# Retention and two MLPs on one core: the constants' load moves from SyncE's queue to ScalarE's

## The chip, the cores and the metric

The kernel runs on one core of one Trainium2 chip. The metric is the device time of one execution, in microseconds (us). Three runs of the kernel before took 550.88, 551.44 and 550.36 us; the median is 550.88 us. A further execution was profiled, and all rows below come from that one.

## The reference, cut to what matters

A decaying linear attention ("retention") runs over 2 batches, 8 heads, 768 steps of width 64. Its output, reshaped to 1536 tokens by 512, goes through two MLPs of width 2048.

```python
gamma = 1.0 - 2.0 ** (-5.0 - np.arange(H))           # one decay per head
for t in range(S):
    state = gamma * state + einsum('bhd,bhe->bhde', k[:, :, t], v[:, :, t])
    y[:, :, t] = scale * einsum('bhd,bhde->bhe', q[:, :, t], state)
x = y.transpose(0, 2, 1, 3).reshape(B * S, H * D)
h = x @ w_in                                          # first MLP
x = (h * tanh(softplus(h))) @ w_out
h = x @ w_in2                                         # second MLP
out = (h * cos(h)) @ w_out2
```

## The kernel before, in words

The retention is cut into 6 chunks of 128 steps, each for both batches. For a chunk TensorE (PE) forms the scores of queries against keys (`att_scores`, L465), VectorE (DVE) multiplies them by a decay mask (`att_mask`, L469, tile `p`), and PE multiplies the result by the values (`att_out`, L506). A running state joins the chunks (`att_update` L479, `att_state` L490, `att_inter` L516); its values come scaled from ScalarE (ACT) and GpSimd (POOL) (`att_vd`, L447 and L444, tile `vd`). ACT then writes the high part of the chunk's output (L526) and a copy of it (L535), and DVE the low part (L538). Everything after that, from 44 us of the trace on, is the matmuls of the two MLPs, each done in three products of high and low parts (L621, L579, L649).

The masks are not loaded. A small tensor of 184 numbers a partition, `consts`, is loaded into the tile `few` (L1040), and the tables of powers grow from it by doublings: DVE makes the mask of 128 x 1024 (`att_mask_grow`, L1051 and L1054, then `att_mask_upper`, L1064), POOL copies the decays that `vd` needs (`att_dec`, L1067) and grows the table for the queries (`att_decq_grow`). All of that waits for the landing of `few`. Beside it, from 1.06 us on, PE runs 24 matmuls on zeros (`start_up`, `zeros`, L1075) ahead of the first scores.

All transfers were issued on SyncE's queue (SP), in a fixed order: `few` first, then queries and keys of chunk 0 (one transfer for each batch, 512 KB), its values (256 KB for each batch), queries and keys of chunk 1, and so on (`chunk_loads`, L419). A transfer waits, on SP, for the landing of the one eight places ahead of it. ACT's first instruction is a table load that the first activation (L1082) brings with it.

The order of the rest is worked out when the program is built: `Plan` holds each operation with a cost and what it needs, goes through them from the end and from the start, and emits the instructions of each engine in the order of the best of 12 rounds. Operations with the engine `None` take no time in it; in the rounds, SP's first operation begins at 2.6, and another engine may use a transfer 2.2 after its operation's end. So the cost and the place that `load_consts` is given there decide when the plan believes the mask and the loads to be there.

Of the kernel before, what the change touches and what calls it, by code (L numbers as in the profile page):

```python
# [88 lines left out]
class Plan:  # L89
# [24 lines left out]
    def op(self, engine, cost, fn, *args, needs=(), uses=(), new=None):  # L114
        n = len(self.ops)
        uses = list(uses)
        before = set(needs)
        reuse = []
        for key, bufs, *tag in [] if new is None else new if isinstance(new, list) else [new]:
            line = self.lines.setdefault(tag[0] if tag else key[0], [])  # L120
            if line:
                before.add(self.owner[line[-1]])
            if len(line) >= bufs:
                reuse.append(line[-bufs])
            line.append(key)
            self.owner[key] = n
            uses.append(key)
        for key in uses:
            if self.owner.get(key, n) != n:
                before.add(self.owner[key])  # L130
            self.users.setdefault(key, set()).add(n)
        if engine in self.given:
            before |= {self.last[engine]} if engine in self.last else set()
            self.last[engine] = n
        att = fn.__name__.startswith("att") or fn.__name__ in ("start_up", "zeros", "load_consts")
        self.ops.append(dict(engine=engine, cost=cost, fn=fn, args=args, before=before, reuse=reuse, att=att, due=(fn.__name__, *args[:1]) in self.DUE or (fn.__name__,) in self.DUE))
        return n
# [125 lines left out]
def retention_two_mlps(ctx: ExitStack, tc: tile.TileContext, qkv, w1i, w1o, w2i, w2o, consts, out):  # L263
    nc = tc.nc
# [476 lines left out]
    op = plan.op  # L741
# [295 lines left out]
    def load_consts():  # L1037
        t = g_p.tile([128, 2, 2, BLK], F32R, tag="g2", name="few").rearrange("p a b c -> p (a b c)").bitcast(F32)
        few_t.append(t)
        nc.sync.dma_start(out=t[:, 0:184], in_=consts[:, 0:184])  # L1040
        upper = t[:, 512 : 512 + C]
        nc.gpsimd.memset(upper, 1.0)
        nc.gpsimd.affine_select(
            out=upper, in_=upper, pattern=[[1, C]], compare_op=ALU.is_ge, fill=0.0, base=0, channel_multiplier=-1
        )
# [38 lines left out]

    at["close"] = op(None, 0.0, nothing)
    at["ret"] = op(None, 0.0, nothing)
    op("PE", 5.5, start_up)
    load = op("SP", 0.4, load_consts, new=("few", 1, "g2"))
    qk, v, k = (0, 1024), (1024, 1536), (1536, 2048)
    for c, cuts in (  # L1090
        (0, qk), (0, v), (1, qk), (0, k), (1, v), (2, qk), (1, k), (3, qk), (2, v), (2, k), (4, qk), (3, v), (3, k),
# [209 lines left out]
```

## Time and profile before

| | |
|---|---|
| median of three runs | 550.88 us (550.36 to 551.44) |
| the profiled execution's own time | 551.34 us |
| its span, first to last instruction | 549.6 us |
| PE busy | 543.3 us (99%) |
| DVE, ACT, POOL busy | 395.3, 315.7, 195.7 us |
| granted TensorE clock | 0.999 of full speed |
| bytes moved | 49.33 MB, mean 90 GB/s |

The profiled execution is 1.74 us longer than its span; that is what lies around the first and last instruction. All three engines beside PE have idle time, PE has 6.3 us of it. The rows further down show where in the span that idle time lies, and what the transfers do at the start. A row's time is counted from the span's start.

### The profile page before, as it was taken

The page shows a single profiled execution, that of the slowest core. Times are in us where ns is not written, and L with a number is a line of the kernel's source. Part 1 is how long each engine was busy: PE and PEld are TensorE (multiplying, and loading weights), DVE is VectorE, ACT ScalarE, POOL GpSimd, SP SyncE. Part 2 cuts the span into 40 slices and gives each one's busy share as a digit, 9 for nine tenths or more (in the row PEclk, how much of TensorE's full clock was granted, in tenths as well). Part 3 has the DMA queues.
Part 4 walks back from the last instruction along what each step waited for, and adds up shares of the span by engine and source line. Part 5 has one row for each costly group of instructions (what it writes and reads, how often), then busy time and mean ns, then how long its engine had stood idle before and what let it go on. Part 6 is the DMA issues. An engine that isn't in the chain of part 4 may idle for free.

```text
span 549.6 us, 7462 instructions
## 1 busy us (share of the span) xinstructions
PE 543.3 (99%) x2962; PEld 451.8 (82%) x2962; DVE 395.3 (72%) x450; ACT 315.7 (57%) x423; POOL 195.7 (36%) x171
## 2 busy tenths in 40 slices
PE   9989999999999999999999999999999999999997
PEld 7888888888888888888888888888888888888886
DVE  5789997776676756385798893978487884978452
ACT  4475646264323404334188978899577867686460
POOL 6772205536341316143223324441514333422000
PEclk9999999999999999999999999999999999999999
DMA  8982420242222220241001312042202301020103
GB/s 287 410 347 78 154 76 1 76 153 78 76 78 76 78 76 2 76 154 40 38 0 43 130 58 76 1 153 78 77 1 78 134 20 76 1 77 1 76 35 118
DMA packets 16162, 49.33 MB, mean 90 GB/s; under 512 B 1792, under 2 KB 2176, under 8 KB 16128
## 3 DMA queue, kind: packets, MB, share of 16 engines
q1 hardware_dynamic: 16128, 48.86, 23.7%
q8 instruction: 23, 0.38, 0.3%
q14 instruction: 11, 0.09, 0.0%
HBM read 45.71 MB, written 3.15 MB: 89 GB/s over the span
## 4 chain that ended last, share of the span: by engine, by line
PE 95%; DVE 1%; DMA 1%; ACT 1%; issue 0%; SPq 0%; DVEq 0%; ACTq 0%
PE bank L649 48%; PE bank L579 26%; PE bank L621 18%; PE bank L506 2%; DMA qkv<-qkv_dram 1%; PE bank L465 1%; PE bank L516 1%; PE bank L479 1%; DVE p L469 0%; ACT vd L447 0%; DVE x L538 0%; DVE mag L334 0%; ACT y L535 0%; ACT x L526 0%; SPq L419 0%
## 5 line engine op out<-in xcount | busy, mean ns | idle before, releaser
L649 PE MATMUL bank<-g,wo 128*128 128x512 f32 x576 | 134.0, 389 | 0.0
L649 PE MATMUL bank<-wo,g 128*128 128x512 f32 (+1 forms) x588 | 133.5, 385 | 0.0
L649 PEld LDWEIGHTS bank<-wo,g 128*128 128x128 f32 x588 | 108.9, 188 | 22.0
L649 PEld LDWEIGHTS bank<-g,wo 128*128 128x128 f32 x576 | 108.1, 188 | 22.4
L621 PE MATMUL bank<-x,wi 128*128 128x512 f32 x432 | 99.4, 389 | 0.0
L621 PEld LDWEIGHTS bank<-x,wi 128*128 128x128 f32 x432 | 81.0, 188 | 16.9 <-issue 0.2
L579 PE MATMUL bank<-x,wi 128*128 128x512 f32 x270 | 66.1, 389 | 0.0
L579 PE MATMUL bank<-S,T 128*128 128x512 f32 x270 | 66.1, 389 | 0.0
L374 POOL TENSOR_TENSOR raw<-mag 128x512 f32<-128x512 f32 x14 | 19.4, 1385 | 127.2 <-DVE mag L355 53.5
L719 DVE TENSOR_TENSOR acc<-bank,acc 128x1024 f32<-128x1024 f32 x35 | 42.7, 1221 | 28.9 <-PE bank L649 28.9
L363 POOL TENSOR_TENSOR wo<-mag,wo 128x512 fp32r<-128x512 f32 x28 | 37.7, 1368 | 71.8 <-ACT wo L349 71.8
L703 DVE TENSOR_TENSOR g<-bank,g 128x1024 fp32r<-128x1024 f32 x40 | 48.9, 1222 | 18.0 <-ACT g L699 17.8
L579 PEld LDWEIGHTS bank<-x,wi 128*128 128x128 f32 x270 | 50.6, 188 | 10.6
L579 PEld LDWEIGHTS bank<-S,T 128*128 128x128 f32 x270 | 50.7, 188 | 10.5
L587 ACT COPY U<-bank 128x512 f32<-128x512 f32 x45 | 26.5, 589 | 54.9 <-PE bank L579 54.7
L392 POOL TENSOR_TENSOR T<-raw,T 128x512 fp32r<-128x512 f32 x28 | 36.5, 1327 | 51.8 <-ACT T L388 51.8
L363 POOL TENSOR_TENSOR wi<-mag,wi 128x512 fp32r<-128x512 f32 x28 | 42.6, 1535 | 32.6 <-ACT wi L349 27.0
L656 ACT ACTIVATE bank<-bank 128x1024 f32<-128x1024 f32 x24 | 24.2, 1009 | 47.5 <-PE bank L621 32.1
L692 DVE TENSOR_TENSOR bank<-angle,bank 128x512 f32<-128x512 f32 (+1 forms) x32 | 30.7, 959 | 28.4 <-ACT angle L688 28.2
L590 DVE TENSOR_TENSOR bank<-bank,U 128x512 f32<-128x512 f32 x45 | 31.3, 697 | 26.3 <-PE bank L579 26.1
L699 ACT CAST g<-bank 128x1024 fp32r<-128x1024 f32 x40 | 40.7, 1016 | 9.3 <-DVE bank L692 8.7
L674 DVE SCALAR_TENSOR_TENSOR angle<-bank,angle 128x512 f32<-128x512 f32 (+1 forms) x32 | 30.5, 953 | 19.9 <-ACT angle L670 19.4
(90 smaller groups left out, 651.9 us busy)
## 6 DMA issues: line engine op xcount, KB each, us to landing
raw<-w1i_dram SPq DMA_DIRECT2D x16, 512.0 KB, 4.1
raw<-w1o_dram SPq DMA_DIRECT2D x16, 512.0 KB, 3.6
raw<-w2i_dram SPq DMA_DIRECT2D x16, 512.0 KB, 3.7
raw<-w2o_dram SPq DMA_DIRECT2D x16, 512.0 KB, 3.7
qkv<-qkv_dram SPq DMA_DIRECT2D x12, 512.0 KB, 7.4
qkv<-qkv_dram SPq DMA_DIRECT2D x22, 256.0 KB, 7.0
out_dram<-acc SPq DMA_DIRECT2D x11, 256.0 KB, 2.0
out_dram<-acc SPq DMA_DIRECT2D x2, 128.0 KB, 1.7
```

The source lines that it names most:

```text
L363: eng.tensor_sub(out=w[:, :, 1], in0=w_all_of(it, single)[:, ns].bitcast(F32), in1=w[:, :, 0].bitcast(F32))
L392: nc.gpsimd.tensor_sub(out=t[:, :, 1], in0=t_of(it)[:, part], in1=t[:, :, 0].bitcast(F32))
L579: nc.tensor.matmul(ps, lhs, rhs, start=(not more and kk + i == 0), stop=(kk == 1 and i == last), skip_group_check=True)
L587: nc.scalar.copy(out=copies[0][:, n], in_=bank[:, WINO_BANK["d"], :])
L590: nc.vector.tensor_add(out=bank[:, WINO_BANK[to], :], in0=bank[:, WINO_BANK[of], :], in1=copies[0][:, n])
L621: nc.tensor.matmul(h, w[:, f % 2, a, kk * 128 : (kk + 1) * 128], x[:, b, kk, :], start=(a + b + kk == 0), stop=(a == 1 and kk == KD - 1),)
L649: nc.tensor.matmul(ps, lhs, rhs, start=(n == 0), stop=(n == 3 * GF - 1))
L674: nc.vector.scalar_tensor_tensor(out=a, in0=h, scalar=INV_2PI, in1=a.bitcast(I32), op0=ALU.mult, op1=ALU.subtract)
L692: nc.vector.tensor_mul(out=h, in0=a, in1=h)
L699: nc.scalar.copy(out=g_t[k][:, :, 0, :], in_=h_of(k))
L703: nc.vector.tensor_sub(out=g[:, :, 1, :], in0=h_of(k), in1=g[:, :, 0, :].bitcast(F32))
L719: nc.vector.tensor_add(out=acc, in0=o_of((m * NG + G, j, p)), in1=acc)
```

## The change

`load_consts` issues the load of `few` on ACT's queue instead of SP's. In the plan it becomes an operation without an engine and without a cost, ahead of `start_up`, which is made to need it; ACT issues the transfer ahead of its first activation. The operation on SP that the consumers of `few` wait for stays in the plan as an empty one of cost 0.0.

```diff
     def load_consts():
...
-        nc.sync.dma_start(out=t[:, 0:184], in_=consts[:, 0:184])
+        nc.scalar.dma_start(out=t[:, 0:184], in_=consts[:, 0:184])
         upper = t[:, 512 : 512 + C]
...
-    op("PE", 5.5, start_up)
-    load = op("SP", 0.4, load_consts, new=("few", 1, "g2"))
+    first = op(None, 0.0, load_consts, new=("few", 1, "g2"))
+    op("PE", 5.5, start_up, needs=[first])
+    load = op("SP", 0.0, nothing, uses=["few"])
```

On ACT, at the start of the program (`few` is the tile of the constants, `spare` and `quarter` are single columns that only serve to bring the table):

```order
-L1296 UNCONDITIONAL_BRANCH [waits barrier_Pool_Activation_PE_DVE_SP_release]
+L1297 UNCONDITIONAL_BRANCH [waits barrier_Pool_Activation_PE_DVE_SP_release]
+L1040 DMA few<-consts_dram 128x184
 L1082 ACT_TABLE_LOAD
 L1082 ACTIVATE spare<-quarter 128x1 [waits DVE_49]
```

ACT now issues the transfer before its table load, and waits for nothing but the barrier at the program's start.

On SP, at the start of the program (`qkv` of 128x1024 is queries and keys of chunk 0 for one batch, of 128x512 its values):

```order
-L1296 UNCONDITIONAL_BRANCH [waits barrier_Pool_Activation_PE_DVE_SP_release]
-L1040 DMA few<-consts_dram 128x184
+L1297 UNCONDITIONAL_BRANCH [waits barrier_Pool_Activation_PE_DVE_SP_release]
 L419 DMA qkv<-qkv_dram 128x1024 x2
 L419 DMA qkv<-qkv_dram 128x512 x2
```

Every load of `qkv` moves up by one place; the order among them is the same.

On DVE, in the stretch in which the first MLP begins (`mag` and `raw` are steps in splitting a weight, `x` is the low part of an output of the last chunks):

```order
 L355 SCALAR_TENSOR_TENSOR raw<-raw,mag 128x512 [waits DVE_49]
 L318 TENSOR_SCALAR mag<-raw 128x512 [waits DMAHW5_49]
+L324 TENSOR_SCALAR mag<-mag 128x512 [waits DVE_49]
 L538 TENSOR_TENSOR x<-bank,x 128x4x128 [waits DMAHW3_49,DMAHW1_49,DMAHW7_49,DMAHW0_49,Activation_49]
-L324 TENSOR_SCALAR mag<-mag 128x512 [waits DVE_49]
 L328 TENSOR_SCALAR mag<-mag 128x512 [waits DVE_49]
 L363 TENSOR_TENSOR wi<-raw,wi 128x512 [waits Activation_49]
```

One clamp of a weight (L324) now stands ahead of one low part of `x` (L538). PE's and POOL's orders are the same as before.

## Rows read from the trace of the kernel before

**Rows 1.** The page's head, and its chain that ended last, by engine.

```profile
span 549.6 us, 7462 instructions
PE 95%; DVE 1%; DMA 1%; ACT 1%; issue 0%; SPq 0%; DVEq 0%; ACTq 0%
```

**Rows 2.** Stretches: start:end, length, busy us by engine, clock, DMA share, GB/s.

```profile
0.00:15.00 15.00, 13.78 (x170) 11.22 (x172) 9.30 (x22) 6.67 (x19) 9.79 (x21) 1.00 0.86 297
15.00:44.00 29.00, 27.23 (x573) 24.30 (x567) 23.35 (x38) 15.67 (x45) 20.65 (x20) 1.00 0.87 342
44.00:100.00 56.00, 56.00 (x251) 46.40 (x248) 51.37 (x67) 32.12 (x39) 15.59 (x12) 1.00 0.23 84
100.00:300.00 200.00, 200.00 (x884) 165.62 (x883) 137.09 (x135) 82.94 (x97) 75.07 (x59) 1.00 0.18 67
300.00:500.00 200.00, 200.00 (x883) 165.53 (x882) 151.31 (x167) 157.26 (x204) 72.02 (x58) 1.00 0.19 69
```

**Rows 3.** The chain that ended last, its beginning: start us, us, what.

```profile
0.81 0.37 SPq L1040
...
1.24 0.41 SPq L419
...
2.17 6.41 DMA qkv<-qkv_dram
...
8.66 2.02 ACT vd L447 x8
...
12.11 0.49 ACT y L535
...
14.43 1.29 DVE p L469 x2
...
15.77 1.09 PE bank L506 x14
```

**Rows 4.** Timeline of the first 17 us, all engines: start us, us, instruction, [idle before].

```profile
0.80 1.28 ACT L1082 ACT_TABLE_LOAD   x1 [0.80 <-PEq L1290]
...
2.10 0.30 ACT L1082 ACTIVATE spare<-quarter 128x1 f32<-128x1 f32 x1
2.75 0.17 DVE L1051 COPY cst<-few 128x8 f32<-128x8 f32 x1 [1.73 <-DMA few<-consts_dram]
...
3.27 3.92 POOL L1054 TENSOR_TENSOR cst<-cst,few 128x4 f32<-128x4 f32 x7
5.49 1.23 DVE L1064 TENSOR_TENSOR cst<-cst,few 128x1024 f32<-128x1024 f32 x1
...
6.00 2.06 PE L465 MATMUL bank<-qkv 64*128 64x128 f32 x32
7.20 2.49 DVE L469 TENSOR_TENSOR p<-bank,cst 128x512 f32<-128x512 f32 x4 [0.48 <-PE bank L465]
...
8.64 0.61 POOL L444 TENSOR_TENSOR vd<-qkv,cst 128x256 f32<-128x256 f32 x1 [1.45 <-DMA qkv<-qkv_dram]
8.66 2.02 ACT L447 ACTIVATE vd<-qkv,cst 128x64 f32<-128x64 f32 x8 [6.27 <-DMA qkv<-qkv_dram]
...
8.98 1.97 PE L506 MATMUL bank<-p,qkv 128*64 128x128 f32 x32
...
11.53 0.58 ACT L526 CAST x<-bank 128x512 fp32r<-128x512 f32 x1
```

**Rows 5.** Transfers issued in 0.8:1.2, then in 1.24:1.65: KB, us to landing.

```profile
few<-consts_dram SPq DMA_DIRECT2D x1, 92.0 KB, 1.9
...
qkv<-qkv_dram SPq DMA_DIRECT2D x1, 512.0 KB, 4.2
```

**Rows 6.** Stretches of the first transfers, columns as in rows 2.

```profile
1.80:2.40 0.60, 0.60 (x5) 0.41 (x4) 0.00 (x0) 0.58 (x2) 0.00 (x0) 1.00 0.92 204
2.40:2.60 0.20, 0.20 (x3) 0.14 (x2) 0.00 (x0) 0.00 (x0) 0.00 (x0) 1.00 0.17 61
2.60:2.80 0.20, 0.20 (x3) 0.14 (x2) 0.05 (x1) 0.00 (x0) 0.02 (x1) 1.00 0.41 164
2.80:5.40 2.60, 2.60 (x14) 1.85 (x13) 2.34 (x8) 0.00 (x0) 2.12 (x8) 1.00 1.00 279
...
8.60:20.00 11.40, 11.13 (x201) 9.71 (x202) 7.48 (x13) 5.95 (x20) 9.72 (x10) 1.00 1.03 412
```

**Rows 7.** Timeline of 44 to 66 us, DVE and then PE, columns as in rows 4.

```profile
44.70 0.69 DVE L538 TENSOR_TENSOR x<-bank,x 128x512 fp32r<-128x512 f32 x1
45.30 0.42 DVE L324 TENSOR_SCALAR mag<-mag 128x512 f32<-128x512 f32 x1
...
43.99 22.06 PE L621 MATMUL bank<-x,wi 128*128 128x512 f32 x96
```

## The prediction

> **What bounds the kernel.** I read the page's head and chain first [rows 1]: of a span of 549.6 us, 95% of the chain that ended last is PE. The stretches [rows 2] then say where anything can be won at all. From 44 to 500 us PE is busy 56.00 of 56.00, 200.00 of 200.00 and 200.00 of 200.00 us: it never waits there. Its idle time lies ahead of that: 1.22 us of the first 15 us (1.06 us of it before its first matmul) and 1.77 us of the 29 us up to 44 us. So a shift of the moment at which PE enters the first MLP, 44 us, goes through to the end one for one, and nothing behind it adds to it. The question is by how much that moment moves.
>
> The beginning of the chain [rows 3] says what sets it: the load of `few` is issued on SP at 0.81, the first queries and keys behind it at 1.24, the first values at 2.17, and these land at 8.57 or so (2.17 + 6.41). ACT scales them from 8.66, copies the first outputs until 12.60 (12.11 + 0.49), DVE makes the low part and the masked scores of chunk 1 until 15.72, and PE goes on at 15.77. The timeline [rows 4] shows the same from the engines: ACT sat idle for 6.27 us before 8.66, until that transfer landed. The landing of the constants stands on the chain only through the 0.43 us (1.24 - 0.81) by which its issue holds SP up. DVE waits for it until 2.75 and then grows the mask until 6.72 (5.49 + 1.23), but after that it waits another 0.48 us, for PE's first scores [rows 4].
>
> **What the change removes: one issue on SP.** Every load of queries, keys and values is issued 0.43 us earlier. How much earlier the values land has two bounds. At most 0.43 us, when the transfers follow their issues. At least 0: both before and after, the first bytes can flow at the same time (the constants' issue at 0.81 becomes that of queries and keys), and the same 92 KB have to pass the same engines ahead of the values, now beside instead of before. A price below zero I leave out: the bytes ahead of the values are the same. Once the stream is steady, from 8.6 to 20 us, it runs at 412 GB/s [rows 6]; at that rate the 92 KB cost 0.22 us. I take 0.43 - 0.22 = 0.21 us, since the engines were only 0.17 and 0.41 busy in 2.40:2.60 and 2.60:2.80, and a part of the 92 KB will fit into such a hole.
>
> The chain then moves by that 0.21 us as a whole. ACT's `vd` follows the landing. Its low limit is PE: the first masked product runs from 8.98 to 10.95 whatever the values do, because PE comes to it from its zeros and scores without a wait. ACT needs its end only for the copy at 11.53, which has 11.53 - 10.95 = 0.58 us of room; 0.21 us fits.
>
> **What it adds: an issue on ACT.** An issue lasted 0.37 us on SP [rows 3]. On ACT the trace shows none; from nothing to several times as long it costs nothing, for ACT finishes its start at 2.40 (2.10 + 0.30) and has 6.27 us until the values land [rows 4]. The table load, 1.28 us from 0.80, moves behind the issue. Cost 0; the cover would have to lose 6 us before it showed.
>
> **What it moves: the landing of the constants.** Before, they had the transfer engines to themselves and landed 1.9 us after their issue [rows 5]. Now they are issued at the same moment (ACT's first work began at 0.80, SP's at 0.81) and share the engines with 512 KB of queries and keys. Call the delay d. At the least it is 0. At the most the constants land with the queries and keys, 4.2 us after the issue [rows 5], at 5.0 instead of 2.75: d = 2.3 us. If the 128 rows of both transfers pass strictly in turn, 92 + 512 = 604 KB have to flow from 1.80 on at the 279 GB/s of 2.80:5.40 [rows 6], which is 2.2 us, until 4.0. Add the 0.5 us that the constants needed before, from their last byte (92 KB at 204 GB/s from 1.80, so 2.25) to 2.75, and they land at 4.5: d = 1.75 us. I take less, d = 0.8 us: queries and keys moved little in their first 0.4 us (61 and 164 GB/s in 2.40:2.80), and in such a slow start most of the constants can pass.
>
> The price of d is read from the room behind it. DVE's first masked scores wait 0.48 us for PE after the mask is done. They end at 9.69 (7.20 + 2.49); PE needs the last of them only for the second half of its product, at 9.97 (halfway from 8.98 to 10.95): 0.28 us more. The product's end has 0.58 us of room against the old time of ACT's copy. The sum is 0.48 + 0.28 + 0.58 = 1.34 us: with d under 1.34 - 0.21 = 1.13 us the gain above is whole, at d = 1.34 us it is gone, and above that the kernel is slower by d - 1.34. POOL's table ends at 7.19 (3.27 + 3.92) and its next work started at 8.64, so 1.45 us of room there. At d = 0.8 us all of it is covered: price 0.
>
> **The swap on DVE.** L324 now runs ahead of one L538, which starts some 0.4 us later than 44.70 [rows 7]. PE is then in a row of 96 matmuls of 22.06 us, and the tile in question, that of the last two chunks, is used last in it. Price 0; without that cover it would be L324's own 0.42 us.
>
> **Sum.** -0.21 + 0 + 0 + 0 = -0.2 us. The profiled execution would have a span of 549.4 us instead of 549.6, and with the 1.74 us around it 551.1 instead of 551.34. Its own time lies 0.46 us above the median of the three runs, 550.88, so the median becomes 550.7 us.
>
> **Rivals.**
> First, the constants come late and the kernel gets slower. The mechanism is the sharing above, its place DVE's mask, and it decides from a landing at 2.75 + 1.34 = 4.1 us on. For it: the two transfers start together, and queries and keys are slow at first (4.2 us for 512 KB), so each row of the constants may wait for a slow one. Against it: the small load among the early rows. Rows in strict turn give 1.75 - 1.34 = +0.4 us, so 551.3 us; the upper bound gives 2.3 - 1.34 = +1.0 us, so 551.8. The Trainium skill bears on this (DMA: Bandwidth & Descriptors, section on queues, rings and completion order): each transfer engine goes round the queues that have work for it, a packet from each. By that rule the constants lose the place at the head that one queue gave them; by rows in turn it makes 551.3 us. No row of before shows two data queues at work, so the trace neither confirms nor denies it.
>
> Second, the transfers are bound by their bytes from 1.80 on, and nothing moves: the values land at 8.57 as before, 550.9 us. For it: the engines were 0.92 busy in 1.80:2.40 and 1.00 in 2.80:5.40 [rows 6]. Against it: the hole between. The same page (section on issuing engines that are not separate DMA queues) says that a second issuing engine only saves the sequencer's issue time, which is this result or at best the 0.43 us; the hole in the trace speaks for a part of it.
>
> Third, the second queue has a cost outside the instructions, in the 1.74 us around the span. No row gives a price for it; a doubling would be 552.6 us. Nothing in the trace speaks for it.
>
> **How the numbers follow.** Forecast (0.05 to 0.45 us faster) 0.50; late constants 0.28; nothing moves 0.17; the third rival 0.05. A measurement of this kernel tells some 0.2%, 1.1 us, from no change. The forecast and the second rival lie within that, and so does the first one, up to its bound of +1.0 us; its chance beyond that, with most of the third rival's, makes slower by more than 0.2% 0.07. Faster by more would need five times the forecast, more than SP's whole issue: 0.02. Within: 0.91. The three runs of before spread by about half a microsecond to each side. So the range goes from 550.0 (0.43 us gained, and that spread) to 551.8 (the bound of the late constants).
>
> **What would show it.** Right: SP's first row is L419 at about 0.81; ACT's `vd` starts at 8.4 to 8.5 instead of 8.66; DVE's copy from `few` starts before 4.1, likely near 3.5; PE's L506 of chunk 1 goes on at about 15.5, and L621 begins near 43.8. The step on the stream is wrong if `vd` still starts at 8.66 or is earlier by more than 0.43 us. The step on the constants is wrong if DVE's first masked scores start after 8.5; if then PE shows a wait in the product that began at 8.98, the first rival has it. A span like before with a longer own time would be the third.

## The result, and the profile after

| | before | changed |
|---|---|---|
| median | 550.77 us (549.37 to 551.44, 6 runs) | 553.62 us (552.57 to 554.27, 6 runs) |
| ratio to before, 95% interval | | 1.0051 [1.0037, 1.0065] |
| the profiled execution's own time, span | 551.34, 549.6 us | 552.62, 550.9 us |

The kernel became 0.5% slower, 2.85 us by the medians. The forecast was 0.2 us faster, and the time lies above the range, which ended at 551.8. The six runs of the changed kernel fall into two groups: 552.57 and 552.62 us at a mean clock of 1.000 and 0.999, and four from 553.58 to 554.27 at 0.996 or 0.997. No run of the kernel before whose clock is on record shows less than 0.999. The profile below is of the upper clock, so it shows only the first part of the loss. The executions of the kernel before also spread over two groups, 549.8 to 550.3 and 551.0 to 551.8 us in one set of ten, at the same clock, and its profile is of the upper one; what the experiments say on that follows behind e18.

The head and the chain, against [rows 1]: DVE's share has grown from 1% to 3%, and ACT is gone.

```profile
span 550.9 us, 7462 instructions
...
PE 96%; DVE 3%; DMA 1%; issue 0%; DVEq 0%
```

The stretches, against [rows 2]: PE's busy time falls by 0.68 us in the first 15 us (13.78 to 13.10) and by 0.48 us from there to 44 us (27.23 to 26.75). Behind that PE is busy without a gap, as before.

```profile
0.00:15.00 15.00, 13.10 (x130) 10.08 (x131) 7.76 (x20) 6.61 (x19) 9.57 (x21) 1.00 0.86 314
15.00:44.00 29.00, 26.75 (x576) 24.61 (x576) 24.65 (x38) 15.73 (x46) 20.82 (x20) 1.00 0.86 333
44.00:100.00 56.00, 56.00 (x279) 46.28 (x276) 51.38 (x69) 32.13 (x39) 15.63 (x12) 1.00 0.21 77
```

The chain's beginning, against [rows 3], is another one. It starts with the constants, goes through DVE's mask (L1054, L1064) and its masked scores (L469), and PE goes on at 17.31 instead of 15.77. ACT's `vd` is no longer in this part of it.

```profile
0.80 4.50 DMA few<-consts_dram
...
8.07 1.24 DVE cst L1064
...
9.40 2.50 DVE p L469 x4
...
17.31 0.76 PE bank L506 x9
```

The timeline, against [rows 4]. ACT's `vd` starts at 7.87 instead of 8.66, so the queries, keys and values do come earlier, by 0.79 us. But DVE's copy from `few` starts at 5.33 instead of 2.75, the mask is done at 9.30, and the masked scores follow without a wait, 2.20 us later than before. PE has done its 8 zeros by 9.57 and waits for them, 0.57 us and then 0.17.

```profile
0.80 0.40 ACTq L1040 DMA_DIRECT2D few<-consts_dram  x1
0.81 15.93 SPq L419 DMA_DIRECT2D qkv<-qkv_dram  x20
1.24 1.28 ACT L1082 ACT_TABLE_LOAD   x1 [1.24 <-PEq L1291]
5.33 0.17 DVE L1051 COPY cst<-few 128x8 f32<-128x8 f32 x1 [4.30 <-DMA few<-consts_dram]
7.87 2.03 ACT L447 ACTIVATE vd<-qkv,cst 128x64 f32<-128x64 f32 x8 [5.04 <-DMA qkv<-qkv_dram]
9.40 2.48 DVE L469 TENSOR_TENSOR p<-bank,cst 128x512 f32<-128x512 f32 x4
10.15 0.43 PE L506 MATMUL bank<-p,qkv 128*64 128x128 f32 x2 [0.57 <-DVE p L469]
10.75 2.28 PE L506 MATMUL bank<-p,qkv 128*64 128x128 f32 x30 [0.17 <-DVE p L469]
```

The two transfers issued in 0.8:1.2, against [rows 5] (KB, us to landing): the constants need 4.5 us instead of 1.9, as long as the 512 KB beside them.

```profile
qkv<-qkv_dram SPq DMA_DIRECT2D x1, 512.0 KB, 4.3
few<-consts_dram ACTq DMA_DIRECT2D x1, 92.0 KB, 4.5
```

The packets of the two queues say how (q1 is SP's, q10 ACT's; packets, MB, share). First the stretch 1.7:2.3, then 2.3:3.3, then 3.3:4.3. Both loads were issued within 0.01 us, but until 2.3 only rows of queries and keys flow. From then on the rows of both go about one for one, 50 to 36 and 61 to 69, and a row of 4 KB stands ahead of each row of 736 bytes.

```profile
q1 hardware_dynamic: 18, 0.07, 56.0%
...
q1 hardware_dynamic: 50, 0.20, 72.2%
q10 hardware_dynamic: 36, 0.03, 15.7%
...
q1 hardware_dynamic: 61, 0.23, 71.1%
q10 hardware_dynamic: 69, 0.05, 16.6%
```

The prediction weighed a rule of the Trainium skill (DMA: Bandwidth & Descriptors, section on queues, rings and completion order): each transfer engine goes round the queues, a packet from each, with 9 to 17 descriptors as the typical packet. The turns agree with these rows; the size of a turn does not, for here it is about one row of each queue.

Against [rows 6]: the engines were 0.73 busy in 1.80:2.40 (0.92 before) and 0.99 at 341 GB/s in 2.80:5.40 (1.00 at 279). Against [rows 7]: the swap of L324 and L538 stands there and costs PE nothing; PE's L621 begins at 45.27 instead of 43.99.

```profile
46.11 0.43 DVE L324 TENSOR_SCALAR mag<-mag 128x512 f32<-128x512 f32 x1
46.45 0.68 DVE L538 TENSOR_TENSOR x<-bank,x 128x512 fp32r<-128x512 f32 x1
```

**The second place.** Between 17.31 (1.54 us late) and 34.12 (L465 of the last chunk, against 33.82 before: 0.30 us late) most of the delay is made up. Then 1.28 us are there again. The stretch has work of its own on DVE: the split of the first weight (L324, L328, L334, L355). Behind it stands the low part of an earlier output (L538), and PE's next product (L506) is written into the bank that L538 reads, so PE waits for it. Before, on DVE, POOL and PE:

```profile
33.50 0.42 DVE L324 TENSOR_SCALAR mag<-mag 128x512 f32<-128x512 f32 x1
33.95 0.77 DVE L328 TENSOR_SCALAR mag<-mag 128x512 uint32<-128x512 uint32 x1
34.76 0.98 DVE L334 SCALAR_TENSOR_TENSOR mag<-raw,mag 128x512 uint32<-128x512 uint32 x1
35.77 1.64 DVE L355 SCALAR_TENSOR_TENSOR raw<-raw,mag 128x512 uint32<-128x512 uint32 x1
37.34 0.68 DVE L538 TENSOR_TENSOR x<-bank,x 128x512 fp32r<-128x512 f32 x1
...
33.82 1.37 POOL L444 TENSOR_TENSOR vd<-qkv,cst 128x256 f32<-128x256 f32 x2 [1.13 <-DMA qkv<-qkv_dram]
35.15 1.72 POOL L452 TENSOR_TENSOR qd<-qkv,cst 128x512 f32<-128x512 f32 x1
36.95 2.95 POOL L455 TENSOR_TENSOR qd<-qkv,cst 64x512 f32<-64x512 f32 x2
...
38.07 1.09 PE L506 MATMUL bank<-p,qkv 128*64 128x128 f32 x16 [1.17 <-DVE x L538]
```

After:

```profile
33.82 0.78 DVE L324 TENSOR_SCALAR mag<-mag 128x512 f32<-128x512 f32 x1
34.63 0.72 DVE L328 TENSOR_SCALAR mag<-mag 128x512 uint32<-128x512 uint32 x1
35.38 1.65 DVE L334 SCALAR_TENSOR_TENSOR mag<-raw,mag 128x512 uint32<-128x512 uint32 x1
37.06 1.64 DVE L355 SCALAR_TENSOR_TENSOR raw<-raw,mag 128x512 uint32<-128x512 uint32 x1
38.62 0.68 DVE L538 TENSOR_TENSOR x<-bank,x 128x512 fp32r<-128x512 f32 x1
...
33.70 1.37 POOL L444 TENSOR_TENSOR vd<-qkv,cst 128x256 f32<-128x256 f32 x2
35.02 1.45 POOL L452 TENSOR_TENSOR qd<-qkv,cst 128x512 f32<-128x512 f32 x1
36.55 3.28 POOL L455 TENSOR_TENSOR qd<-qkv,cst 64x512 f32<-64x512 f32 x2
...
39.35 1.09 PE L506 MATMUL bank<-p,qkv 128*64 128x128 f32 x16 [2.15 <-DVE x L538]
```

The same four instructions take 4.79 us instead of 3.81 (a few us later in the same profile, with POOL idle, 0.42, 0.43, 0.69 and 0.69), and PE's wait for L538 behind them grows from 1.17 to 2.15 us. DVE's start is 0.32 us later (33.82 against 33.50) and the split 0.98 longer: together 1.30, the delay of L621 and of the span. So the reading to be tested: the late constants shift DVE against POOL, whose start hardly moves (33.70 against 33.82), so that its products lie beside the whole split; and something lowers the clock in more than half of the runs.

### The profile page after: what moved, and what is told of

Read it like the earlier page. It is cut to its first block, busy times and chain, and to the rows that moved or that the text cites. A ratio compares the mean times of both kernels' runs of the same rounds, so it can differ in the third digit from the quotient of the medians.

```text
span 550.9 us, 7462 instructions
## 1 busy us (share of the span) xinstructions
PE 543.5 (99%) x2962; PEld 451.8 (82%) x2962; DVE 396.3 (72%) x450; ACT 315.9 (57%) x423; POOL 195.8 (36%) x171
## 4 chain that ended last, share of the span: by engine, by line
PE 96%; DVE 3%; DMA 1%; issue 0%; DVEq 0%
PE bank L649 47%; PE bank L579 26%; PE bank L621 18%; PE bank L506 2%; PE bank L465 1%; DMA few<-consts_dram 1%; DVE p L469 1%; PE bank L516 1%; PE bank L479 1%; DVE cst L1054 0%; DVE mag L334 0%; DVE x L538 0%; DVE cst L1064 0%; DVE mag L328 0%; DVE mag L324 0%
## 5 line engine op out<-in xcount | busy, mean ns | idle before, releaser
L621 PE MATMUL bank<-x,wi 128*128 128x512 f32 x432 | 99.3, 389 | 0.0
L621 PEld LDWEIGHTS bank<-x,wi 128*128 128x128 f32 x432 | 81.0, 188 | 16.9 <-issue 0.2
L334 DVE SCALAR_TENSOR_TENSOR mag<-raw,mag 128x1024 uint32<-128x1024 uint32 (+1 forms) x36 | 44.5, 1236 | 0.6
```

The lines of the kernel that those rows point to most:

```text
L334: nc.vector.scalar_tensor_tensor(out=a, in0=high, scalar=0xC0000000, in1=a, op0=ALU.bitwise_and, op1=ALU.bitwise_or)
L621: nc.tensor.matmul(h, w[:, f % 2, a, kk * 128 : (kk + 1) * 128], x[:, b, kk, :], start=(a + b + kk == 0), stop=(a == 1 and kk == KD - 1),)
```

## The experiments

Three explanations were set against each other. One, lateness alone: the delay of the constants, less the room behind it, goes through. Two, the collision: the delay costs much more where it brings DVE's split beside POOL. Three, the clock: TensorE's waits are followed by a lower granted clock. Each ratio is to runs of the kernel before on the same chip (medians from 550.01 to 550.76 us); a comparison of one experiment with another mostly crosses chips.

**Is the loss there again?** e1_changed_again is the changed kernel, unaltered.

> The changed kernel once more, unaltered. Its profile showed a span 1.3 us longer than before, but the median of its six runs is 2.85 us longer, and four of the six show a granted clock of 0.996 or 0.997 with spans of 551.9 to 552.6 us; the two at 0.999 and 1.000 have 550.9. Theory A (the late constants alone): every run near 552.6, clock 0.999. Theory B (the late constants, 1.3 us, and on top of them a stretch at the lower clock in most runs, 1.1 to 1.7 us): two groups of runs, about 552.6 and 553.9, the second at 0.996 or 0.997. Theory C (the second queue itself costs time, wherever the constants land): no prediction of two groups.

553.27 us, ratio 1.0061 [1.0039, 1.0083]. Again two groups: three runs of 552.59 to 552.72 at 0.999, three of 553.82 to 555.43 at 0.994 to 0.996. Over all 12 runs, 5 at 0.999 or above have a mean of 552.64 and 7 below it one of 554.11: the lower clock costs 1.47 us where it comes (the run at 0.994, 555.43 us, lost about twice that). e9_before_again is the kernel before, profiled once more.

> The kernel before, unaltered, for a second profile of it. Its 56 runs so far fall into two groups, 42 at 549.2 to 550.7 us and 14 at 551.3 to 552.2, all at a clock of 0.999 or 1.000, and the profile that the forecast was read from (551.34) is of the upper one. Theory D: a profile from the lower group shows DVE's split (L324 to L355) starting before POOL's products at 33.7 and taking less than the 3.8 us of the first profile, and PE's wait near 37 shorter than 1.17 us; a profile from the upper group shows them as in the first.

550.63 us, 0.9998 [0.9984, 1.0012]; its profile (551.55) is of the upper group again and looks like the first: split of 3.84 us, PE wait of 1.20.

**The second queue, or the late landing?** e2_second_on_sp is the kernel before with everything on SP, the constants behind the first queries and keys. e3_act_ahead keeps them on ACT, and holds SP's first load back behind a memset of one column of its target. e7_short_rows cuts that load into two of 256 KB, with rows of 2 KB.

```diff
 # e2: in the kernel before (the first two loads leave the list that follows)
+    chunk_loads(0, 0, 1024, 0)
     load = op("SP", 0.4, load_consts, new=("few", 1, "g2"))
+    chunk_loads(0, 0, 1024, 1)
...
 # e3: in start_up of the changed kernel
+        att_tile(0, 0)
+        nc.vector.memset(att[0, 0][:, 0:1], 0.0)
 # e7: the first load in two, in the changed kernel
+    chunk_loads(0, 0, 512, 0)
+    chunk_loads(0, 512, 1024, 0)
+    chunk_loads(0, 0, 1024, 1)
...
```

> All loads on SP's queue again, ACT issues none, but the constants are the second transfer, behind the first 512 KB of queries and keys. Theory A and B (their landing is what costs): the constants land at 5 us or later, DVE's first masked scores start near 9.3, and the time is that of the changed kernel, 552.6 to 553.9. Theory C (the second queue): the time of before, 550.8.

> The constants stay on ACT's queue; SP's first load is made to wait for one more small fill by DVE into its tile, so that it is issued at about 1.05 instead of 0.81, and ACT's issue at 0.80 is alone for 0.25 us. If the rows of both queues are simply taken in turn by each transfer engine, the head start lets about half of the constants' rows pass, the last of them still wait behind rows of 4 KB, and the landing is between 3.5 and 5 us: 551.0 to 552.5. If the descriptors of the two queues are made one transfer after the other (in the changed kernel the first row of the constants moved at 2.31, the first of queries and keys at 1.81), the constants go first as a whole, land at 2.7 to 2.9, and the time is that of before, 550.6 to 550.9. Theory C: as slow as the changed kernel.

> The changed kernel with the first 512 KB transfer of queries and keys cut into two of 256 KB, so that the rows beside which the constants' 736-byte rows have to pass are 2 KB instead of 4 KB. If each transfer engine takes a row from each queue in turn: the constants pass beside half as many bytes and land 0.8 to 1.3 us earlier than in the changed kernel (5.3), near 4.2, and the time falls by 0.5 to 1.5 us. If the constants simply come behind what SP had issued by then (two queues, one line), or share by bytes: they land at 5.1 to 5.5, and the time stays near 553.

e2: 552.63 us, 1.0043 [1.0025, 1.006], with the copy from `few` at 5.32 and L469 at 9.39, as in the changed kernel. No second queue is there, and the loss is: it is the landing. e3: 550.02 us, 1.0004 [0.999, 1.0018]. SP's load went out at 1.08, 0.28 us after the constants, and in 1.7:2.3 the picture is turned round: 94 packets of the constants to 4.

```profile
q10 hardware_dynamic: 94, 0.06, 77.1%
q1 hardware_dynamic: 4, 0.02, 16.0%
```

They land at 3.28, between the two landings that had been expected (2.7 to 2.9, or 3.5 and later), and the loss is gone although the second queue is there. e7: 551.44 us, 1.0019 [1.0003, 1.0034]; landing 4.77, between the two expectations (near 4.2, and 5.1 or later). Shorter rows beside it bring 0.5 us of the landing and some 2 us of the time.

**Where does the delay turn into time?** e5_split_later lets the planner put the first weight's split behind the last masked scores; e6 and e8 do the same to the kernel before and to e3. e10_dve_delay delays the split in the kernel before by two memsets.

```diff
 # e5, e6, e8
+    hold(at["clamp", ("i", 0, 0), 0], at["p", 5, 1, 1])
 # e10: ahead of L324
+        if it == ("i", 0, 0) and not ns.start:
+            for _ in range(2):
+                nc.vector.memset(mag_t[it][:, 1].bitcast(F32), 0.0)
```

> The changed kernel, with the first weight's split on DVE (L324, L328, L334, L355, which stood ahead of the masked scores of the last chunk) held until behind them. In its profile these four took 4.8 us (0.78, 0.72, 1.65, 1.64) beside POOL's products from 33.7 to 39.8, against 2.9 us in the run with ACT ahead (0.42, 0.43, 1.10, 0.99), and PE waited 2.15 us behind them. Theory D (the delay of the constants is a loss of about 1 us at 33 us, and the larger part comes from the split then falling into POOL's work, and from the lower clock after PE's long wait): PE's wait at 37 to 39 goes, no run shows 0.996, and the time falls to 549 to 550.5, near or below that of before. Theory A (the late constants pass through one for one, and the split only happens to stand there): 552 or more.

> The kernel before with the same hold, the constants first on SP. Theory D: what the delay of the constants costs by itself is the difference between the run above and this one, 0.7 to 1.3 us, and this one is faster than before by 0.3 to 1.5 us, since its split (3.8 us in the profile of before) collides in part too: 548.5 to 549.7. Theory A: the difference between the two is the whole 2.7 us of the changed kernel.

> Both mended: ACT's issue with the head start of 0.28 us (constants at 3.3 us) and the split held back. Theory D: the same as the kernel before with the hold, within 0.3 us, 548.3 to 549.7, and faster than before. If the earlier issue on SP is worth anything (in the run with ACT ahead the first queries and keys were issued at 1.08 instead of 1.24, the values landed at 8.57 as before), it shows as more than 0.3 us against that kernel; I expect nothing.

> The kernel before with two fills of 512 columns on DVE ahead of the first weight's split, into a part of a tile that is written later anyway: some 0.5 to 1 us of DVE time at 33 us, and nothing else. The constants land as in the kernel before. Theory D: the split is pushed into POOL's products as in the changed kernel, and PE waits 2 us or more; the loss is larger than the added DVE time, 1.5 to 3 us against before, and some runs show 0.996. Theory A (only what comes late from the mask counts): the loss is at most the added DVE time, 0.5 to 1 us, and no run shows 0.996.

e5: 551.68 us, 1.0028 [1.0017, 1.0038]; e6: 550.73, 1.0004 [0.9992, 1.0015]; e8: 551.22, 1.0008 [0.9997, 1.0018]. Without a split in the way the changed kernel is 0.95 us slower than before with the same edit, not 2.9. None of the three reached the range that had been expected (e5 550.5 at most, e6 and e8 549.7), and three of e5's 12 runs were still at 0.996 or 0.997. e6 and e8 did not gain on the kernel before: the planner also moved POOL's `vd` behind `qd`, and PE waited for that (0.44, 0.74 and 0.55 us in the profiles of e5, e6 and e8). e10: 554.54 us, 1.0063 [1.0043, 1.0084], all six runs at 0.994 to 0.997. Some 1.1 us of delay cost 3.8 us, the lower clock in every run included, with the constants on time. Its split takes 0.36, 1.38, 1.64 and 1.64 us, PE's wait behind it is 3.58. So the loss can be made in the kernel before, by delaying DVE alone.

e13_pool_out takes POOL's part away: of the changed kernel's `vd` of chunk 4 POOL scales one head in place of four, and its `qd` of chunk 5 only four columns.

```diff
+            h = slice(0, 1 if c == 4 else H // 2)
...
+        if c == 5:
+            nc.gpsimd.tensor_mul(out=qd_of(c, b)[:, :, 0:4], in0=q[:, :, 0:4], in1=decq[:, :, 0:4])
+            return
```

> The changed kernel, leaving out most of POOL's work between 33.7 and 39.8 us: its share of the scaled values of chunk 4 is cut to one of four heads and the scaled queries of chunk 5 to 4 of 128 columns (0.4 of 6.1 us of work stays). DVE's work is untouched. Theory D: DVE's split, 4.8 us in the changed kernel, takes 2.2 to 2.6 us, PE's wait of 2.15 us falls under 0.3 us, no run shows 0.996, and the time falls by 2 to 2.6 us against the clean runs of the changed kernel (552.7), to 550 to 550.7, though the constants still land at 5.3. Theory A, or DVE slow for another reason (the transfers, ACT's work beside it): the split stays above 4 us and the time at 552 or more.

550.9 us, 1.0013 [1.0002, 1.0024]; the constants land at 5.29 as before, and its split takes 0.45, 0.43, 0.69 and 0.69 us. That names POOL, but with work left out. Five of its 12 runs were at 0.997, where none had been expected. The last three leave out nothing. DVE sets one column for each batch (128x2) of the tile that POOL's `qd` of chunk 5 writes, right behind the split, so these products start after it: e16_before_pool_later in the kernel before, e17_changed_pool_later in the changed one, e18_ahead_pool_later in e3.

```diff
 # behind L355
+        if it == ("i", 0, 0) and ns.start == 0:
+            nc.vector.memset(att["qd"][:, (NCH - 1) % 2, :, 0, 0:1], 0.0)
```

> The kernel before, with one more instruction on VectorE: a memset of one column of POOL's tile qd right behind the first weight's split (L355). POOL's products for chunk 5 write that tile, so they now start when the split is done instead of beside it. Nothing is left out. Theory (POOL's two-input products beside the split cost it 1 to 2 us, and TensorE waits for what DVE does next): L334 and L355 take 0.69 us each instead of 0.98 and 1.64, the split ends 1.0 to 1.3 us earlier, TensorE's wait behind it falls from 1.2 us to under 0.4 us, and the time is 0.4 to 1.0 us below the kernel before: a ratio of 0.998 to 0.9993. Rival (the split is slow for another reason, such as the transfers that land then): L334 and L355 stay at 0.98 and 1.64, the time stays within 0.2 us of before.

> The changed kernel with the same one memset, so POOL's products for chunk 5 start behind the split. Nothing is left out. Theory: of the 4.79 us of the split the parts L334 and L355 fall from 3.29 to 1.4 us, TensorE's wait near 37 us falls from 2.15 us to 0.3 to 0.6 us, and the runs with the clock at 0.999 come to 550.7 to 551.3 instead of 552.6; with fewer runs of lowered clock behind that wait, the median is 1.5 to 2.5 us under the changed kernel, 0.0 to 0.8 us over the one before. Rival (the late constants cost the 1.5 us of their delay by themselves): 552.0 or more, ratio above 1.002.

> The load on ScalarE's queue with SP's first load held behind a first memset (the version whose constants landed at 3.28 us and whose time was 550.02), with the same memset behind the split. If the split is what TensorE waits for there as well: 549.3 to 549.9, a ratio of 0.998 to 0.9995, and no better than the kernel before with the memset alone, since the values land at the same time in both. If the wait near 37 us had gone already there (0.28 us in its profile): 550.0, no difference from that version.

e17: 550.97 us, 1.001 [0.9999, 1.0021]. Six runs at 1.000 take 550.47 to 550.56, six at 0.997 551.38 to 552.13; fewer of the second kind had been expected. One memset of 0.06 us gives 2.1 us back (552.64 to 550.52, runs of the upper clock on different chips). DVE and then PE in e17:

```profile
35.46 0.69 DVE L334 SCALAR_TENSOR_TENSOR mag<-raw,mag 128x512 uint32<-128x512 uint32 x1
36.18 0.69 DVE L355 SCALAR_TENSOR_TENSOR raw<-raw,mag 128x512 uint32<-128x512 uint32 x1
...
37.54 1.09 PE L508 MATMUL bank<-p,qkv 128*64 128x128 f32 x16 [0.25 <-DVE x L540]
```

The two halves of the split beside POOL fall from 3.29 to 1.38 us and PE's wait from 2.15 to 0.25. L324 and L328 stay at 0.77 and 0.72, still beside POOL's `vd`. The lateness left by itself is 550.52 - 550.03 (the mean of e16) = 0.5 us. e16: 550.09 us, 0.999 [0.9981, 1.0]: L334 takes 0.69 us, L355 still 0.99, since `vd` came later, and the gain, about 1 us at most, is not sure. e18: 549.99 us, 0.9985 [0.9974, 0.9996]. It is faster than both kernels, by 0.2 to 1.4 us against the one before. Its distance from e16 (0.1 us) is within the spread, so the second queue itself shows no gain.

The two groups of the kernel before bear on this. All 23 runs of e16 and e18 are at 550.65 us or below; of the 29 runs of the kernel before beside them, 9 are at 551.04 or above. So its upper group goes too when POOL's products wait for the split: the kernel before seems to pay for the collision in about a third of its executions. No execution of its lower group was profiled; e3's profile, at 549.49 us, has a split of 2.94 us and a PE wait of 0.28 us.

**The clock.** e4_more_zeros puts 20 zero matmuls instead of 8 ahead of the first masked product of the changed kernel; e11_fill_wait puts 20 between the two halves of the masked product of chunk 4, where PE waits at 37 us; e12_fill_both does both. e14_fill_look and e15_fill_look are e11 again, for its profile.

```diff
 # e4, e12
-    op("PE", 0.9, zeros, 8)
+    op("PE", 0.9, zeros, 20)
 # e11, e12
...
+            if (c, b) == (4, 1):
+                op("PE", 0.0, zeros_add, 20)
```

> The changed kernel with 20 instead of 8 matmuls on zeros ahead of the first masked product, so that PE is busy from 8.5 to 10.7 while it waits for the mask; no other order changes. Theory A: no change against the changed kernel, or up to 0.1 us slower. Theory B, with the wait at 9.6 to 10.7 as what lowers the clock: all runs at 0.999, near 552.6, so 1 us faster in the median than the changed kernel; if it is another wait that lowers the clock (2.15 us of PE at 37 to 39), the same two groups as the changed kernel.

> The changed kernel with 20 matmuls on zeros (adding zero to the state's bank) between the two masked products of chunk 4, where PE waits 2.15 us for DVE; PE's other order, and those of DVE, POOL and SP, are the same. If PE's wait there is what lowers the clock for 3.4 us in about half of the runs (both profiles that caught a lowered clock show it fall at 39.3 and 39.8 us, just behind that wait): no run shows 0.996 any more, the runs lie within 552.4 to 552.9, and the median falls by 0.5 to 1.2 us against the changed kernel. If the clock falls for another reason: the same share of runs at 0.996, near 554.

> The changed kernel with both of PE's long waits filled: 20 instead of 8 matmuls on zeros ahead of the first masked product, and 20 between the masked products of chunk 4. If the clock falls after either wait, and each of the two runs so far left one of them open: no run at 0.996, all within 552.4 to 553.2. If it falls for a reason that matmuls on zeros do not mend, or after another wait: a third to a half of the runs at 0.996 or 0.997, near 554.

> The changed kernel with PE's wait at 37 to 39 us filled by matmuls on zeros, once more, for a profile that may catch a run at the lower clock: 3 of its 6 runs were at 0.996 or 0.997. If it is caught, the fall begins near 10 to 13 us (the wait there was not filled) or again near 38 to 40 us (then matmuls on zeros do not help).

> The same kernel as the look before this one, with the same two outcomes: a fall of the clock near 10 to 13 us, or near 38 to 40 us, if a run at the lower clock is caught.

e4: 552.65 us, 1.005 [1.0032, 1.0068], two of 7 runs at 0.996. e11: 553.5 us, 1.0048 [1.0032, 1.0063], three of 6 at 0.996 or 0.997, which had been expected to go. e12: 553.67 us, 1.0059 [1.0042, 1.0075], and none under 0.999; but the zeros themselves cost about 1 us (553.67 against 552.64). e15 (552.81, 1.000) shows nothing; e14 (554.25, 0.997) caught the fall. Its stretches, columns as in [rows 2], the granted clock behind the five busy times:

```profile
6.00:10.80 4.80, 3.11 (x36) 2.19 (x32) 4.41 (x10) 2.13 (x8) 4.30 (x9) 1.00 0.95 353
10.80:14.40 3.60, 3.48 (x30) 3.27 (x30) 1.63 (x4) 1.07 (x2) 3.46 (x4) 0.53 1.05 414
14.40:20.00 5.60, 5.50 (x99) 4.87 (x100) 4.01 (x7) 2.98 (x10) 5.39 (x6) 1.00 1.03 410
```

It begins 0.5 us behind PE's first wait, 1.59 us until 10.32 in that execution (0.57 in the profile of the changed kernel). In e7's profile (554.6) it stands behind the second, 2.23 us until 39.65:

```profile
36.00:39.70 3.70, 1.47 (x26) 1.11 (x22) 3.67 (x4) 3.47 (x12) 3.55 (x3) 1.00 0.89 353
39.70:43.20 3.50, 3.50 (x52) 3.38 (x52) 2.88 (x5) 0.00 (x0) 0.42 (x1) 0.51 0.03 13
```

e4's and e10's profiles show it at that place too, there from the wait's last 0.1 to 0.5 us on. So the clock falls to its lower level, 1.2 GHz, for 3.4 us near the end of one of the two waits, in some runs, and e11 missed because it filled one wait of two. These 3.4 us at half of full speed are 0.003 of the span, which makes the means of 0.996 and 0.997. Which run it meets is not settled: the first profile of the changed kernel waits 2.15 us at the second place without a fall, and e5's waits 1.58 us at the first.

## Why the prediction was wrong

- **What it moves: the landing of the constants** is the step that failed. It took d = 0.8 us, with 2.3 us as the most; the landing at 5.31 makes d = 2.56, and the masked scores start at 9.40, behind the 8.5 that was to show the step wrong. The bound fell short because the constants landed 0.2 us behind the queries and keys, and not with them. I chose 0.8 because queries and keys were slow in their first 0.4 us, "and in such a slow start most of the constants can pass". None passed: until 2.3 us all rows were of queries and keys. Rows in turn, the first rival, was the right mechanism, and its 1.75 was too little: the constants' first row came 0.5 us after the other load's, and 0.3 us stay open.
- **The price of d** failed too. The room was put at 1.34 us, and the first rival's price, d - 1.34, gives 1.2 us with the right d, so 552.1. The runs at full clock are at 552.64, and the median at 553.62. That the two profiled spans differ by 1.3 us, close to that price, is luck: at 17 us PE was 1.54 us late (so the room there was 1.0 us), at 34 us only 0.30, and the split then added 0.98. The room was read from the stretch behind the mask alone. I didn't follow DVE to 34 us, where the split runs beside POOL already in the kernel before and PE waits 1.17 us behind it. Against e16, whose split meets less of POOL's work, the changed kernel at full clock is 2.6 us slower: lateness 0.5 (e17 against e16; e5 against e6 gives 0.95) and the collision 2.1 (changed against e17). A part of the 2.1 the kernel before pays too: its runs beside e16 have a mean of 550.60, 0.57 us over e16's. The lower clock, which the forecast did not have at all, costs 1.47 us in 7 of 12 runs and adds 0.9 us on average. The sum, 3.5, is the distance of the changed kernel's two medians, 553.27 and 553.62, from e16 (3.2 to 3.6; other chips).
- **What the change removes.** The stream gains more than the 0.21 us taken, and more than the bound of 0.43: `vd` starts 0.79 us earlier, so by its own sign this step was wrong as well, and why the gain is that large is not shown. It is worth nothing, since PE now waits for the mask and not for `vd`.
- **What it adds: the issue on ACT** took 0.40 us and cost 0, as forecast. So did **the swap on DVE**.
- **From 44 us on** PE never waits, and the 1.28 us of L621 are the 1.3 us of the span, as forecast.
- **The other rivals.** "Nothing moves" is out by the 0.79 us. A cost outside the span is out: 552.62 - 550.9 = 1.72 us, against 1.74.
- **The chances.** Slower by more than 0.2% had 0.07, since the late constants were priced at 1.0 us at most. A bound taken from one stretch was used as the bound for the kernel.

## What to carry to other kernels

Issue a small load that everything waits for ahead of the big ones, or let them wait for it: on a second queue beside a big load its rows took turns with longer ones here, and 0.28 us of head start (e3) was the whole difference. When a step becomes late, follow each engine that it shifts to the next place where engines meet, since a delay of 0.3 us at DVE's split became 1.3 us in the span. Where VectorE's work with both operands in SBUF stands ahead of a wait of TensorE, keep GpSimd's products away from it; a memset of 0.06 us that makes them wait gave back 2.1 us.

## What was not expected of the hardware

- Two loads issued on two queues within 0.01 us did not start together: rows of the one flowed from 1.81, of the other from 2.31. With 0.28 us between the issues (e3) the order was that of the issues.
- VectorE's instructions with two SBUF operands took 1.65 us beside GpSimd's two-input products and 0.69 without them, one-input ones 0.78 and 0.42. L469, with one operand in PSUM, took 0.62 us each beside them (four from 30.09 in 2.47 us, POOL's products running from 28.48 to 33.62). The Trainium skill (SBUF — State Buffer, section on two separate sides) says that the two engines share one pair of ports, and that whichever starts first holds it for its whole instruction. These rows agree: a DVE instruction lasted as long as the product beside it (1.64 us each).
- Near the end of waits of TensorE of 1.59, 2.23 and 3.58 us (e14, e7, e10) the granted clock went to its lower level for 3.4 us; at ones of 1.58 us (e5) and 2.15 us (the changed kernel's profile) it did not.
